# Pooled attention and a maxout layer on one core: block 7's output stage by seven products, its sums on GpSimd, and a rearranged start

## The chip, the cores and the metric

The kernel runs on one core of a Trainium2 chip. A core has five engines that run side by side, each with its own instruction queue, which it works off in order: TensorE (PE: matrix products, results in the memory PSUM; its weight loads are shown as PEld), VectorE (DVE), ScalarE (ACT), GpSimd (POOL) and SyncE (SP, which issues DMA transfers here). They wait for each other by semaphores. PSUM has eight banks of 128 partitions x 512 float32 columns, which the kernel hands out by tags; SBUF is the memory that the other operands live in.

The metric is the time of one execution in device microseconds. A profiled execution gives the span from its first to its last instruction, and a trace of all instructions in between.

## The reference

```python
def _attn_ref(q, k, v):                      # 8 batches, 8 heads, 576 tokens, 64 columns
    k_p = k.reshape(B, H, Sp, pool, D).mean(axis=3)      # pool = 8, Sp = 72
    v_p = v.reshape(B, H, Sp, pool, D).mean(axis=3)
    scores = scale * np.matmul(q, k_p.transpose(0, 1, 3, 2))
    scores = scores - np.max(scores, axis=-1, keepdims=True)
    attn = np.exp(scores)
    attn = attn / (np.sum(attn, axis=-1, keepdims=True) + 1e-09)
    return np.matmul(attn, v_p)

def _moe_ref(x, w1, w2, w3, w_out):          # 4608 tokens, 512 -> 768 -> 512
    h = np.maximum(np.maximum(x @ w1, x @ w2), x @ w3)
    return h @ w_out

x = attn_out.transpose(0, 2, 1, 3).reshape(B * S, H * D)
out = _moe_ref(x, w1, w2, w3, w_out)         # (4608, 512) float32
```

Keys and values are averaged over groups of eight, so the attention is cheap; most of the work is in the layer behind it.

## The kernel before

**The maths.** The hidden layer is computed as x w1 + max(x (w2 - w1), x (w3 - w1), 0). The first part is linear, so w1 w_out is formed once (`linear`, tile `wm`), and the output is x (w1 w_out) + h w_out with h the maximum. `sub_w` makes the differences of the weights in place (L303), in three parts of 256 columns; `turn_w` transposes w1 for `linear`.

**Attention of a batch.** Queries are transposed (`turn_q` on TensorE for the first three batches, step "T", a DMA transpose in SyncE's queue, for batches 3 to 7, L274); pooled keys are transposed into `kz` ("k"); `scores` gives the scores and ScalarE their exponentials (`et`, L197, steps "s"); `values` multiplies by the pooled values (steps "v", five chunks of tokens per batch), and VectorE divides (`rcp` L247, `xn` L249); `turn_x` transposes the result into `xT` (steps "x"), on TensorE up to batch 2 (L231, then a copy, L235), by a DMA transpose in SyncE's queue from batch 3 on (L225).

**The layer.** The 4608 tokens make nine blocks of 512. For blocks 0 to 5, `hidden(n)` computes two products for each of six groups of 128 hidden rows (`pw`, L330; ScalarE's relu L336, VectorE's maximum L338), in two halves of 256 tokens for the first rows of blocks 0 and 1, and `project(n)` makes four tiles of 128 tokens of the output: four matmuls with `wm` (L370), six with w_out (L374), 512 columns each, a copy (L379) and two stores (L383). Each `yield` in these generators is a slot; a written plan says which attention steps of the next batches go into which slot.

The hidden layers of blocks 6, 7 and 8 are computed by `seven(n)`: Strassen's seven products in Winograd's form, on quarters of 256 tokens and half of the columns, for three groups of rows a, b, c. Step "T" in the order there is `fold_x(n)`, which makes the four sums T1 to T4 of x (L566): VectorE for blocks 6 and 7, GpSimd for block 8. The results are collected by VectorE (L679, L682) and ScalarE (L707, L711). `fold_out` makes the sums of the output weights on GpSimd (L596), one after every second product.

`ORDER` is the written order of the last stage, the weave: "1a" is product 1 for rows a, its n-th appearance being block 6, 7 and 8; "s70" and "v70" are attention steps of batch 7; "F" is one slot of `project`, half an output tile. In it stand ten of the twelve tiles of blocks 5 to 7; one more follows, and then the output of block 8, by `out_seven(8)`: seven products of two times five matmuls of 256 columns (L638), with sums `th` of its hidden rows on VectorE (`fold_h`). Block 7's last tile, in two halves, ends the kernel.

**What sets the order.** Every engine's order is the order of the program's text; nothing reorders it. A step waits for data and for a free buffer: PSUM tags have few buffers ("tr" 1, "pw" 3, "att" 2 with two banks each; in the weave "sc" 2, "pa" 2, "bc" 1, "po" 1, "val" 1). SyncE's queue holds output stores and DMA transposes, GpSimd's holds loads, the poolings of keys and values (L136 to L139) and the sums named above.

**The start.** Before block 0 the first batch's attention is written out by hand: `scores4`, `scores2`, two `values`, two `turn_x`, with `turn_w` and `sub_w` between them and dummy matmuls (`heat`).

Of the kernel before, what the change touches and what calls it, by code (L numbers as in the profile page):

```python
# [14 lines left out]
def kernel(  # L15
# [11 lines left out]
    nc = tc.nc  # L27
# [30 lines left out]
    pools = [stage.enter_context(tc.tile_pool(name="psp", bufs=1, space=PSUM))]  # L58
# [124 lines left out]
    def turn_k(b):  # L183
        pkt = keys(b, ATT if len(pools) == 1 else SC)
        for par, evac in enumerate((nc.vector.tensor_copy, nc.scalar.copy)):
            fill_kz(b, par, 0, H, pkt, evac if b > 2 else nc.vector.tensor_copy)
# [50 lines left out]
    def values(b, c0):  # L237
        tag = ATT if len(pools) == 1 else ("val", 1)
        pav = psum([128, 2, 512], F32, name="pav", tag=tag[0], bufs=tag[1])
        for h in range(H):  # L240
            nc.tensor.matmul(  # L241
                pav[:, h // 4, 65 * (h % 4):65 * (h % 4) + 65],
                ets[b][:, h, c0:c0 + 128], vp_all[:, b, h, :],
                start=True, stop=True)
        pv = pav[:, :, 0:260].rearrange("p g (h e) -> p g h e", e=65)
        rcp = sb3.tile([128, 2, 4], F32, name="rcp", tag="rcp")
        nc.vector.reciprocal(out=rcp, in_=pv[:, :, :, 64])  # L247
        xn = sb3.tile([128, 2, 4, D], F16, name="xn", tag="xn", bufs=6)
        nc.vector.tensor_tensor(  # L249
            out=xn, in0=pv[:, :, :, 0:D],  # L250
            in1=rcp.to_broadcast([128, 2, 4, D]), op=ALU.mult)
        return xn

    CHUNKS = ((0, 0), (128, 0), (256, 0), (384, 0), (448, 64))
    ATT = ("att", 2)
    SC = ("sc", 2)
# [6 lines left out]
    def do(b, steps):  # L263

        for name in steps.split():
            i = int(name[1:] or 0)
            if name[0] in "qQ":
                turn_q(b, *QS[i], nc.vector.tensor_copy if name[0] == "Q"  # L270
                       else nc.scalar.copy, TR)
            elif name[0] == "T":
                qTs[b] = sb2.tile([128, 2 * NG, 128], BF16, name="qT", tag="qT")
                nc.sync.dma_start_transpose(  # L274
                    out=qTs[b], in_=qbs[b].rearrange("p hp t d -> p (hp t d)"))
            elif name[0] == "k":
                turn_k(b)
            elif name[0] == "K":
                fold_k(b, nc.vector)
            elif name[0] == "p":  # L280
                pool_v(b, 4 * i, 4 * i + 4, TR, nc.scalar.copy)
            elif name[0] == "s":
                if i == 0:
                    new_et(b)
                (scores if len(pools) == 1 else scores_flat)(b, i)
            elif name[0] == "d":
                sub_w(i)
            elif name[0] == "w":
                turn_w(i, nc.scalar.copy if i % 2 else nc.vector.tensor_copy)
            elif name[0] == "v":  # L290
                xns[b, i] = values(b, CHUNKS[i][0])
            else:
                turn_x(b, *CHUNKS[i], xns[b, i], ATT if len(pools) == 1 else SC,
                       nc.vector.tensor_copy if name[0] == "X" else nc.scalar.copy)
# [4 lines left out]
    def sub_w(i):  # L299

        part = slice(256 * i, 256 * i + 256)
        for t in w_sb[1:]:
            nc.vector.tensor_tensor(out=t[:, :, part], in0=t[:, :, part],  # L303
                                    in1=w_sb[0][:, :, part], op=ALU.subtract)
# [42 lines left out]
    def hidden(n):  # L347
# [3 lines left out]
        if halves:  # L351
            for c0 in (0, NB // 2):
                for jc in range(3):
                    yield from hidden_part(n, jc, c0, c0 + NB // 2, hT)
# [5 lines left out]
    def project(n):  # L360
        hT = hTs[n]
        for mm in range(4):
            m = 4 * n + mm
            last = m == TOK // 128 - 5
            osb = sb3.tile([128, C], F32, name="osb", tag="osb", bufs=5)
            for c in ((slice(0, C // 2), slice(C // 2, C)) if last else (slice(0, C),)):
                tag = PW if len(pools) == 1 else (PO, SC, PA)[max(0, m - (TOK // 128 - 7))]
# [20 lines left out]
    wm = psum([128, 512], F32, name="wm", tag="tr", bufs=1)  # L388
# [8 lines left out]
    pkp0 = psum([128, 6, D], F32, name="pkp", tag="pw", bufs=3)  # L397
# [24 lines left out]
    turn_q(0, 0, 5, nc.vector.tensor_copy, PW)  # L422
    turn_q(0, 5, 9, nc.scalar.copy, ATT)
    pkt0 = [keys(0, PW) for _ in range(2)]
# [4 lines left out]
    def scores4(h):  # L429
        psc = psum([128, 4, 256], F32, name="psc4", tag="att", bufs=2)  # L430
        for i in range(4):
            score(0, h + i, psc[:, i, :], 0, 0, 4)
        exp(ets[0][:, h:h + 4, 0:256], psc[0:Sp])

    def scores2(h):
        psc = psum([128, 2, 512], F32, name="psc2", tag="att", bufs=2)
# [6 lines left out]
    turn_q(0, 9, 14, nc.vector.tensor_copy, PW)  # L443
    turn_q(0, 14, 18, nc.vector.tensor_copy, PW)
    pool_v(0, 0, 4, PW, nc.vector.tensor_copy)
    scores4(4)
    pool_v(0, 4, 6, PW, nc.vector.tensor_copy)
    pool_v(0, 6, 8, PW, nc.vector.tensor_copy)
    scores2(0)
    xn0 = [values(0, c0) for c0, _ in CHUNKS[:2]]  # L450
    heat(1)
    turn_x(0, 0, 0, xn0[0], PW)
    scores2(2)
    turn_w(0, nc.scalar.copy)
    turn_x(0, 128, 0, xn0[1], PW, nc.vector.tensor_copy)
    sub_w(0)
    scores2(4)
    turn_w(1, nc.vector.tensor_copy)
    scores2(6)


    nc.vector.memset(kz_all[1], 0.0)
    xns[0, 0], xns[0, 1] = xn0

    FOLDS = (3, 4, 5, 6, 7, 8, 9, 11)

    def block(n, plan, parts, folds=()):

        for slot, _ in enumerate(part for stage in parts for part in stage(n)):
# [5 lines left out]
            if folds and slot in FOLDS:  # L475
# [3 lines left out]
    block(0, {0: [(0, "v2")], 1: [(0, "v3 d1")], 2: [(0, "x2")],  # L479
              3: [(0, "x3 w2")], 4: [(0, "v4")], 6: [(0, "x4")],  # L480
              8: [(0, "w3")], 9: [(0, "d2")], 12: [(0, "w4")], 13: [(0, "w5")],
# [3 lines left out]
              32: [(1, "v1 x0")], 33: [(1, "X1 v2")]}, (hidden, project))  # L485
# [7 lines left out]
    def plan1():  # L493
        return {0: [(1, "v3")], 1: [(1, "x2")], 2: [(1, "v4")], 3: [(1, "x3")],
                5: [(1, "x4")],
                6: [(2, "k")], 8: [(2, "q0")], 9: [(2, "q1")], 11: [(2, "q2 s0")],
# [4 lines left out]
                23: [(2, "v4 x3")], 24: [(2, "x4")], 17: [(2, "s6"), (3, "T")]}  # L501

    def plan(n):
# [4 lines left out]
        got[1] = [(b + 1, "T")]  # L508
# [23 lines left out]
    LEAD = {0: [(6, "s0")], 1: [(6, "s1"), (7, "T")], 2: [(6, "s2")], 3: [(6, "s3")],  # L532
# [35 lines left out]
    def fold_x(n):  # L568

        x, t = halves(n), turns(n)  # L570
        for part in ([slice(0, 1), slice(1, 2)] if n == LAST else [slice(0, 2)]):
            fold_t(nc.gpsimd if n == LAST else nc.vector,
# [26 lines left out]
    def fold_h(n):  # L599

        th[n] = ld.tile([128, 4, JH, HALF], F16, name="th", tag="ktFalse")
        h = {i: hTs[n][:, JH * (i // 2):JH * (i // 2) + JH,
                       HALF * (i % 2):HALF * (i % 2) + HALF] for i in range(4)}
        fold_t(nc.vector, h, [th[n][:, i] for i in range(4)])

    def out_seven(n):
# [6 lines left out]
        def store(e, j, c):  # L613
            for u in range(2):
                b, g = divmod(2 * (4 * n + 2 * j) + u, NG)
                dst = out[S * b:S * b + S, :].rearrange("(r g) c -> r g c", g=NG)
                e.dma_start(out=dst[:, GS[g]:GS[g + 2] + 1:4, c],
                            in_=o[64 * u:64 * u + 64, j, :, c])

        def product(i, m):  # L620
            of = "B" if i == 2 else "C" if i in (4, 7) else "A"
            if i in FIRST:
                tag = {"A": PA, "B": SC, "C": BC if m == 0 else SC}[of]
                banks[of, m] = psum([128, 2, HALF], F32, name=f"o{of}", tag=tag[0],
                                    bufs=tag[1])
            p = banks[of, m][:, 0]
            za, zb = PRODUCTS[i]
            for r in range(5):
                c = slice(128 * m, 128 * m + 128)
                if isinstance(zb, str):  # L630
                    z = int(zb[1]) - 1
                    left = turns(n)[:, z, r, c] if r < 2 else th[n][:, z, r - 2, c]
                else:
                    at = HALF * (zb % 2) + 128 * m
                    left = (xT[:, 2 * (zb // 2) + r, NB * n + at:NB * n + at + 128] if r < 2
                            else hTs[n][:, JH * (zb // 2) + r - 2, at:at + 128])
                right = out_s(int(za[1]))[:, r] if isinstance(za, str) else out_w(za, r)
                nc.tensor.matmul(p, left, right, start=(i in FIRST and r == 0), stop=(r == 4),  # L638
                                 skip_group_check=True)
            done.add((i, m))  # L640

            def copy(j, c):
                nc.scalar.copy(out=o[:, j, m, c], in_=p)

            def plus(j, c, p):
                nc.vector.tensor_tensor(out=o[:, j, m, c], in0=o[:, j, m, c], in1=p,
                                        op=ALU.add)

            if i in (1, 5, 6, 3):
                copy(i in (5, 3), lo if i in (1, 3) else hi)  # L650
            elif i == 2:
                plus(0, lo, p)
                if m:
                    store(nc.gpsimd, 0, lo)
            elif i == 4:
                plus(0, hi, p)
                if m:
                    store(nc.sync, 0, hi)
            if i in (5, 7) and (12 - i, m) in done:
                plus(1, hi, banks["C", m][:, 0])  # L660
            if i in (5, 7, 3) and all((z, m) in done for z in (5, 7, 3) for m in range(2)):
                store(nc.sync, 1, slice(0, C))

        return product

    def seven(n):
# [19 lines left out]
        def product(i, g):  # L686
# [3 lines left out]
            if not done:  # L690
                hTs[n] = new_hT()
# [30 lines left out]
        k7 F F T v62 1a 1b F s70 s71 6a 6b 2a 7a s72 v63 5a s73 F 2b 5b 4a s74 3a  # L722
        s75 F s76 7b 1c s77 v64 s78 4b 6c F v70 2c 5c 7c 3b F v71 3c F 4c 1a 1b T F
        v72 2b F 2a 6b 6a 7a F v73 5a F v74 3a 5b 4a F 1c F 6c 7b 3b T F 5c 4b F 7c
        1a 2c 2a 4c 6a 3c F 5a 7a 1b 2b 3a 6b 4a 1c 2c 5b 6c 7b 3b F 4b 5c F 7c 3c F
        4c
    """

    def weave():

        products, seen, sums = {}, {}, fold_out()
        for name in ORDER.split():
            if name == "F":
                next(tiles)
            elif name[0] in "ksvx":
# [34 lines left out]
    tiles = (t for n in range(5, LAST) for t in project(n))  # L770
    weave()
    next(tiles)
    next(tiles)
# [37 lines left out]
```

The softmax here doesn't subtract the row's maximum and nothing guards it: scores larger than these inputs give would overflow.

## Time and profile before

| | |
|---|---|
| median of 13 runs | 238.13 us |
| lowest and highest of them | 233.06 and 243.7 us |
| the profiled execution | 233.06 us |
| its span | 231.2 us |
| granted TensorE clock, mean | 1.000 |

The page's section 2 shows the span in 40 slices, each digit the busy share in tenths:

```profile
PE   7787999999999999999999999999999999999992
DVE  3669756037434342624263336258679887897730
ACT  2356434755774577237723772475686535465330
POOL 7665202999915999999996999910243442920020
DMA  6999999999499868998997899972431537311236
```

A slice is 5.8 us. TensorE is busy nearly everywhere; VectorE is busiest in the weave, from the 28th slice on; GpSimd pools keys and values until the 27th and makes sums after it.

In the lines below, a group is "line engine operation out<-in"; times of windows and of the timeline count from the span's start; square brackets hold an engine's idle time before an instruction and what ended it.

### The profile page before, as it was taken

To read this page: it belongs to the slowest core of one execution; us is meant where nothing else is said; L and a number is where in the kernel's file an instruction comes from. 1 tells how busy PE (TensorE), PEld (TensorE's weight loads), DVE (VectorE), ACT (ScalarE), POOL (GpSimd) and SP (SyncE) were. 2 spreads that over 40 slices of the span, in tenths; PEclk is the share of its full clock that TensorE was granted. 3 is DMA by queue.
4 is the path that set the end of the run, shared out by engine and by line. 5 is a ranking of instruction groups with operands and counts; after the bars stand their busy time and mean duration, and the time that the engine had idled before them with its cause. 6 is when DMAs were issued, how large, how long until landed. Compare 5 with 4: busy or idle time off the path is not lost.

```text
span 231.2 us, 4547 instructions
## 1 busy us (share of the span) xinstructions
PE 221.2 (96%) x1766; PEld 137.0 (59%) x1767; DVE 128.2 (55%) x237; ACT 120.3 (52%) x215; POOL 137.9 (60%) x113
## 2 busy tenths in 40 slices
PE   7787999999999999999999999999999999999992
PEld 2575745557656555545554555455677667786682
DVE  3669756037434342624263336258679887897730
ACT  2356434755774577237723772475686535465330
POOL 7665202999915999999996999910243442920020
PEclk9999999999999999999999999999999999999999
DMA  6999999999499868998997899972431537311236
GB/s 181 205 196 197 212 202 212 177 186 227 72 204 166 177 149 139 183 174 195 148 184 174 152 213 171 152 180 49 79 72 25 112 70 105 70 23 45 67 73 181
DMA packets 47174, 33.53 MB, mean 145 GB/s; under 512 B 27313, under 2 KB 41905, under 8 KB 47153
## 3 DMA queue, kind: packets, MB, share of 16 engines
q0 software_dynamic: 16960, 16.98, 45.7%
q1 hardware_dynamic: 30032, 16.13, 33.7%
q8 instruction: 14, 0.23, 0.4%
q10 hardware_dynamic: 160, 0.13, 0.2%
q14 instruction: 8, 0.06, 0.1%
HBM read 34.60 MB, written 9.44 MB: 190 GB/s over the span
## 4 chain that ended last, share of the span: by engine, by line
PE 88%; DVE 3%; DMA 3%; ACT 1%; issue 1%; POOL 1%; POOLq 0%; DVEq 0%
PE pw L330 26%; PE po L374 18%; PE po L370 12%; PE pA L701 7%; PE psc L192 5%; PE pav L241 4%; PE pC L701 3%; DMA vt<-in_v_dram 3%; PE pm L317 2%; PE oA L638 2%; PE pxt L231 2%; PE pB L701 2%; PE pkt L174 1%; DVE mw L303 1%; PE oC L638 1%
## 5 line engine op out<-in xcount | busy, mean ns | idle before, releaser
L330 PE MATMUL pw<-xT,mw 128*128 128x512 f16 (+1 forms) x336 | 73.1, 349 | 0.3 <-DVE xT L235 0.3
L338 DVE TENSOR_TENSOR hT<-t,pw 128x512 f16<-128x512 f16 (+1 forms) x42 | 25.5, 609 | 39.6 <-ACT et L197 26.9
L374 PE MATMUL po<-mwo,hT 128*128 128x512 f16 (+1 forms) x198 | 46.8, 372 | 0.0
L379 ACT COPY osb<-po 128x512 f32<-128x512 f32 (+1 forms) x32 | 18.5, 579 | 42.0 <-PE po L374 41.2
L330 PEld LDWEIGHTS <-mw 128*128 128x128 f16 x336 | 28.9, 98 | 19.2 <-issue 0.8
L197 ACT ACTIVATE et<-psc 72x576 f16<-72x576 f32 (+2 forms) x54 | 35.3, 660 | 6.3 <-PE psc L192 6.1
L136 POOL TENSOR_TENSOR half<-vt 72x2048 f32<-72x2048 f16 x7 | 28.4, 4061 | 13.8 <-DMA vt<-in_v_dram 13.4
L370 PE MATMUL po<-wm,xT 128*128 128x512 f16 (+1 forms) x132 | 33.0, 372 | 0.0
L336 ACT ACTIVATE t<-pw 128x512 f16<-128x512 f32 (+1 forms) x42 | 22.5, 536 | 15.4 <-PE pw L330 13.6
L249 DVE TENSOR_TENSOR xn<-pav,rcp 128x512 f16<-128x512 f32 x40 | 27.6, 691 | 1.4
L374 PEld LDWEIGHTS <-hT 128*128 128x128 f16 x198 | 18.4, 98 | 16.2
L137 POOL TENSOR_TENSOR half<-half 72x1024 f32<-72x1024 f32 (+1 forms) x13 | 27.2, 2096 | 1.0
L192 PEld LDWEIGHTS <-kz 128*128 128x128 bf16 x191 | 17.5, 98 | 13.7 <-DVE kz L179 0.4
L192 PE MATMUL psc<-qT,kz 128*128 128x320 bf16 (+2 forms) x168 | 22.4, 246 | 0.4 <-DVE kz L179 0.3
L241 PEld LDWEIGHTS <-et 72*128 72x128 f16 x320 | 15.4, 98 | 8.3 <-issue 0.6
L707 ACT CAST pad<-pA 128x512 f16<-128x512 f32 x27 | 15.3, 587 | 8.4 <-PE pA L701 6.0
L136 POOL TENSOR_TENSOR half<-ktFalse 96x1536 f32<-96x1536 f16 x6 | 18.6, 3098 | 0.3
L247 DVE RECIPROCAL rcp<-pav 128x8 f32<-128x8 f32 x40 | 8.2, 204 | 17.8 <-PE pav L241 17.6
L241 PE MATMUL pav<-vp,et 72*128 72x65 f16 x320 | 17.2, 194 | 0.6 <-ACT et L197 0.6
L370 PEld LDWEIGHTS <-xT 128*128 128x128 f16 x132 | 11.9, 98 | 9.0
L682 DVE SCALAR_TENSOR_TENSOR hT<-pad 128x512 f16<-128x512 f16 x18 | 14.4, 810 | 1.8 <-ACT pad L711 1.4
L701 PEld LDWEIGHTS <-sw 128*128 128x128 f16 x144 | 13.7, 98 | 2.7
(102 smaller groups left out, 274.2 us busy)
## 6 DMA issues: line engine op xcount, KB each, us to landing
out_dram<-osb SPq DMA_DIRECT2D x62, 128.0 KB, 2.5
ktFalse<-in_k_dram POOLq DMA_DIRECT2D x7, 576.0 KB, 6.9
qb<-in_q_dram POOLq DMA_DIRECT2D x7, 576.0 KB, 13.9
vt<-in_v_dram POOLq DMA_DIRECT2D x7, 576.0 KB, 11.3
mw<-in_moe_w_dram POOLq DMA_DIRECT2D x9, 256.0 KB, 10.0
ktTrue<-in_k_dram SPq DMA_DIRECT2D x3, 384.0 KB, 5.0
mwo<-in_moe_w_out_dram POOLq DMA_DIRECT2D x1, 768.0 KB, 12.9
qb<-in_q_dram POOLq DMA_DIRECT2D x2, 288.0 KB, 7.8
```

The costliest lines, as they stand in the source:

```text
L136: e.tensor_tensor(out=f, in0=t[:, :, 0:4, :], in1=t[:, :, 4:8, :], op=ALU.add)
L137: e.tensor_tensor(out=f[:, :, 0:2, :], in0=f[:, :, 0:2, :], in1=f[:, :, 2:4, :], op=ALU.add)
L192: nc.tensor.matmul(out, kz_all[b % 2][:, f % 2, h, :], qTs[b][:, n + i0:n + i1, 64 * (h % 2):64 * (h % 2) + 64], start=True, stop=True)
L197: nc.scalar.activation(out=out, in_=in_, func=FT.Exp, scale=1.0 / 64.0)
L241: nc.tensor.matmul(pav[:, h // 4, 65 * (h % 4):65 * (h % 4) + 65], ets[b][:, h, c0:c0 + 128], vp_all[:, b, h, :], start=True, stop=True)
L249: nc.vector.tensor_tensor(out=xn, in0=pv[:, :, :, 0:D], in1=rcp.to_broadcast([128, 2, 4, D]), op=ALU.mult)
L330: mm = nc.tensor.matmul(pw, w_sb[wi][:, kc, bass.ts(jc, 128)], xT[:, kc, col], start=(kc == 0), stop=(kc == KCH - 1))
L336: nc.scalar.activation(out=t, in_=pw, func=FT.Relu)
L338: nc.vector.tensor_tensor(out=hT[:, jc, c0:c1], in0=t, in1=pw, op=ALU.max)
L370: nc.tensor.matmul(po, xT[:, kc, bass.ts(m, 128)], wm_sb[:, kc, c], start=(kc == 0), stop=False)
L374: nc.tensor.matmul(po, hT[:, jc, bass.ts(mm, 128)], wo_sb[:, jc, c], start=False, stop=(jc == JCH - 1))
L701: mm = nc.tensor.matmul(p[:, w], a[:, kc, bass.ts(g, 128)], b[:, kc, :], start=(i in FIRST and w + kc == 0), stop=(w + kc == 2), skip_grou ...
```

## The change

Five things are changed together.

1. Block 7's output is also made by `out_seven`, within the weave, with both halves of 128 tokens in one call ("o1" to "o7"), so that its copies and additions cover 512 columns. `project` makes blocks 5 and 6 alone, and block 6's last tile, in two halves, ends the kernel.
2. GpSimd makes block 7's sums: `fold_x(7)`, and `fold_h(7)` (step "H") in twelve instructions of 128x256. Block 8's hidden rows get a tile of their own.
3. `ORDER` is written anew, and block 5's weight sums (`FOLDS`) come a slot earlier.
4. The query transposes "T" of batches 4 to 7 come three slots earlier.
5. The start is rearranged: its own pool of PSUM ("att" with three buffers, "one" with two), closed before `turn_w`; scores and values in another order; the first subtraction in pieces; `turn_w`, `sub_w` and the clearing of the second `kz` in later slots of block 0; one dummy matmul less. Block 0's hidden halves come in another order, v3 of batch 1 moves from block 1 into block 0, q0 of batch 2 a slot earlier, and `turn_x` of batch 1 uses the tag "tr".

```diff
     def values(b, c0):
-        tag = ATT if len(pools) == 1 else ("val", 1)
+        tag = (ATT0, ATT, ("val", 1))[len(pools) - 1]
...
-                turn_x(b, *CHUNKS[i], xns[b, i], ATT if len(pools) == 1 else SC,
+                turn_x(b, *CHUNKS[i], xns[b, i], TR if b == 1 else ATT,
...
-            for c0 in (0, NB // 2):
-                for jc in range(3):
-                    yield from hidden_part(n, jc, c0, c0 + NB // 2, hT)
+            parts = {}
+            for p in ("00 00 01 01 10 10 11 11 02 02 12 12" if n == 0 else
+                      "00 00 01 01 02 02 10 10 11 11 12 12").split():
+                if p not in parts:
+                    c0 = int(p[0]) * NB // 2
+                    parts[p] = hidden_part(n, int(p[1]), c0, c0 + NB // 2, hT)
+                next(parts[p])
+                yield
...
     scores2(0)
-    xn0 = [values(0, c0) for c0, _ in CHUNKS[:2]]
-    heat(1)
-    turn_x(0, 0, 0, xn0[0], PW)
+    xn0 = [values(0, CHUNKS[0][0])]
     scores2(2)
+    xn0.append(values(0, CHUNKS[1][0]))
+    turn_x(0, 0, 0, xn0[0], ONE)
+    scores2(4)
+    sub_w(0, 0, 1, (1,))
+    turn_x(0, 128, 0, xn0[1], ONE, nc.vector.tensor_copy)
+    sub_w(0, 0, 1, (2,))
+    sub_w(0, 1, 2)
+    scores2(6)
+    first.close()
+    pools.append(stage.enter_context(tc.tile_pool(name="psp", bufs=1, space=PSUM,
+                                                  reuse_waits="tile")))
     turn_w(0, nc.scalar.copy)
-    turn_x(0, 128, 0, xn0[1], PW, nc.vector.tensor_copy)
-    sub_w(0)
-    scores2(4)
-    turn_w(1, nc.vector.tensor_copy)
-    scores2(6)
-
-
-    nc.vector.memset(kz_all[1], 0.0)
...
-    block(0, {0: [(0, "v2")], 1: [(0, "v3 d1")], 2: [(0, "x2")],
-              3: [(0, "x3 w2")], 4: [(0, "v4")], 6: [(0, "x4")],
-              8: [(0, "w3")], 9: [(0, "d2")], 12: [(0, "w4")], 13: [(0, "w5")],
+    block(0, {0: [(0, "v2")], 1: [(0, "v3")], 3: [(0, "x2 x3 w1 v4")], 6: [(0, "x4 d1")], 9: [(0, "w2")], 10: [(0, "d2")], 11: [(0, "w3")], 12: [(0, "w4")], 14: [(0, "w5 z")],
...
-              32: [(1, "v1 x0")], 33: [(1, "X1 v2")]}, (hidden, project))
+              32: [(1, "v1 x0")], 33: [(1, "X1 v2 v3")]}, (hidden, project))
...
-        got[1] = [(b + 1, "T")]
+        got[18] = [(b + 2, "T")]
...
     def fold_h(n):
 
-        th[n] = ld.tile([128, 4, JH, HALF], F16, name="th", tag="ktFalse")
         h = {i: hTs[n][:, JH * (i // 2):JH * (i // 2) + JH,
                        HALF * (i % 2):HALF * (i % 2) + HALF] for i in range(4)}
-        fold_t(nc.vector, h, [th[n][:, i] for i in range(4)])
+        if n < LAST:
+            t = ld.tile([128, 4, JH, HALF], F16, name="th", tag="ktFalse")
+            th[n] = [t[:, i] for i in range(4)]
+            for r in range(JH):
+                fold_t(nc.gpsimd, {i: h[i][:, r] for i in h}, [t[:, i, r] for i in range(4)])
+            return
...
-        k7 F F T v62 1a 1b F s70 s71 6a 6b 2a 7a s72 v63 5a s73 F 2b 5b 4a s74 3a
-        s75 F s76 7b 1c s77 v64 s78 4b 6c F v70 2c 5c 7c 3b F v71 3c F 4c 1a 1b T F
-        v72 2b F 2a 6b 6a 7a F v73 5a F v74 3a 5b 4a F 1c F 6c 7b 3b T F 5c 4b F 7c
-        1a 2c 2a 4c 6a 3c F 5a 7a 1b 2b 3a 6b 4a 1c 2c 5b 6c 7b 3b F 4b 5c F 7c 3c F
-        4c
+        k7 1a F F 2a T 1b v62 s70 F s71 s72 6a F s73 v63 5a 7a s74 s75 v64 F s76 4a
+        s77 3a s78 6b 2b 7b 1c v70 2c 5b T F 6c v71 3b F 5c 4b F v72 7c 3c 1a F 1b
+        4c v73 2a 2b 6b 6a F v74 5a 7a F 3a F T 1c 4a 5b 2c 6c 7b 3b F 5c 4b F 1a 7c
+        2a 3c 6a 4c H 1b 2b 5a 6b 7a 3a o1 1c 4a o2 5b 6c 7b 2c o6 4b 3b 5c o5 7c o7
+        4c 3c o3 o4
...
+            elif name == "H":
+                fold_h(LAST - 1)
+                outs = out_seven(LAST - 1)
+            elif name[0] == "o":
+                outs(int(name[1]), 0, 1)
...
-    tiles = (t for n in range(5, LAST) for t in project(n))
+    tiles = (t for n in range(5, LAST - 1) for t in project(n))
     weave()
-    next(tiles)
-    next(tiles)
     outs = out_seven(LAST)
     fold_h(LAST)
```

## The prediction, made before the changed kernel ran

> **What bounds the kernel now.** I read the page first, then a table of windows cut at the stages, then the TensorE timeline of the windows that have idle time, then GpSimd's timeline in the last stage.
>
> From the page:
>
> ```profile
> span 231.2 us, 4547 instructions
> PE 221.2 (96%) x1766; PEld 137.0 (59%) x1767; DVE 128.2 (55%) x237; ACT 120.3 (52%) x215; POOL 137.9 (60%) x113
> PE 88%; DVE 3%; DMA 3%; ACT 1%; issue 1%; POOL 1%; POOLq 0%; DVEq 0%
> ```
>
> TensorE is the bound, and the chain that ended last runs through it for 88%. Where the other 12% lie, the windows tell (us, then busy time and count of PE, PEld, DVE, ACT, POOL, then clock, DMA share, GB/s):
>
> ```profile
> 0.00:10.00 10.00, 7.64 (x48) 3.69 (x48) 4.76 (x10) 1.74 (x2) 7.83 (x17) 1.00 0.88 192
> 10.00:26.00 16.00, 13.19 (x170) 10.52 (x168) 12.23 (x29) 9.47 (x18) 8.84 (x12) 1.00 1.40 198
> 46.00:60.00 14.00, 13.27 (x145) 9.63 (x143) 8.15 (x18) 7.87 (x17) 13.68 (x9) 1.00 1.01 197
> 60.00:161.70 101.70, 101.70 (x737) 53.95 (x735) 44.03 (x82) 56.02 (x96) 79.33 (x44) 1.00 0.90 160
> 161.70:217.10 55.40, 55.40 (x452) 39.22 (x450) 45.00 (x75) 31.18 (x56) 20.24 (x28) 1.00 0.33 65
> ```
>
> From 60 to 217.1 us TensorE never rests, so there only less matrix work helps, and each new wait costs its full length. Idle time stands in the prologue and at two places near 52 and 59 us. The timeline (start, length, line, in brackets the idle time before and its releaser):
>
> ```profile
> 15.82 0.40 PE L231 MATMUL pxt<-identh,xn 128*128 128x128 f16 x4 [0.15 <-DVE xn L249]
> 17.96 0.38 PE L309 MATMUL pwt<-identh,mw 128*128 128x128 f16 x4 [0.59 <-ACT w1T L310]
> 21.01 0.40 PE L231 MATMUL pxt<-identh,xn 128*128 128x128 f16 x4 [0.22 <-DVE xn L249]
> 22.18 0.40 PE L231 MATMUL pxt<-identh,xn 128*128 128x128 f16 x4 [0.34 <-DVE xn L249]
> 24.88 0.40 PE L231 MATMUL pxt<-identh,xn 128*128 128x128 f16 x4 [0.36 <-DVE xn L249]
> 52.52 0.60 PE L330 MATMUL pw<-xT,mw 128*128 128x256 f16 x4 [0.26 <-DVE xT L235]
> 59.45 0.44 PE L167 MATMUL pqt<-ident,qb 128*128 128x128 bf16 x5 [0.34 <-ACT qT L169]
> ```
>
> The ends of matmuls are modelled some 0.17 us late, so the true hole is that much longer: 0.42 us at 52.52 and 0.51 at 59.45, from start to start less the work.
>
> **The output stage of block 7.** Removed: four tiles of 10 matmuls of 512 columns. In the chain six of them (L374) take 1.29 to 1.30 us, so 40 x 0.216 = 8.64 us. Added: 7 products x 2 x 5 = 70 matmuls of 256 columns; ten of them (L638) take 1.09 us in the chain, so 70 x 0.109 = 7.62. Gain 1.02 us, all in a stage without idle time. ScalarE gives up four copies of 512 columns and gets four of the same size (0.585 us each, L379): nothing. VectorE gives up block 7's four token sums (0.41 to 0.89, L566) and gets three additions of 512 columns from PSUM (0.69, as L679): nothing within 0.4 us, and it is busy 45.0 of 55.4 us. The new stores (8 DMAs for 8) stand ahead of block 8's and go out some 10 us before the end. Block 6's last tile ends the kernel in two halves as block 8's last tile did, so the 4.1 us from TensorE's last matmul to the span's end stay. One cover is thin: block 8's hidden sums (VectorE, 0.55 each) now queue behind o4's addition (0.69), so T2 is there 0.2 + 0.69 + 1.1 = 2.0 us after o4; TensorE has four plain products (2.18) until then. Without it the end moves by what is missing. The earlier weight sums in block 5 fall where VectorE is busy 44.0 of 101.7 us: nothing.
>
> **GpSimd's new work** is the price. It gets eight sums for block 7's inputs and twelve for its hidden rows (th), 20 instructions of 128x256, behind the weight sums and block 8's eight sums, in one queue. What such a row costs:
>
> ```profile
> 197.09 0.67 POOL L566 TENSOR_TENSOR pad<-xT 128x256 f16<-128x256 f16 x1
> 197.83 1.00 POOL L566 TENSOR_TENSOR pad<-xT,pad 128x256 f16<-128x256 f16 x1
> 199.42 1.12 POOL L566 TENSOR_TENSOR pad<-xT,pad 128x256 f16<-128x256 f16 x1
> 203.12 0.67 POOL L596 TENSOR_TENSOR so<-mwo,so 128x256 f16<-128x256 f16 x1
> ```
>
> From 197.09 to 203.12 it did eight: 6.03 us, 0.754 each; undisturbed they follow each other at 0.63. The long two overlap VectorE's maximum (L682). First the inputs' sums: from v70 to block 7's product 6b, which reads T2, TensorE has 13 products of 0.435, four half-tiles (4.32) and four values groups (1.08), 11.1 us; the transpose of v70 lands some 4.5 us after v70's start, six sums take 4.5, with 0.4 between, so 1.7 us are to spare: no cost. Then the chain to product 6 of the new stage ("o6" in the order), counted from v74. TensorE: v74 0.27, 30 products 13.05, half-tiles 2 x 0.865 + 2 x 1.295 = 4.32, o1 and o2 2.18, so o6 would start at 19.8 us and read the last th piece at 20.3. GpSimd: xn is there at 1.4, but SyncE's two stores stand ahead until 2.05 (0.79 for ScalarE's copy, 1.2 for two issues, as at 183.23); the transpose lands in 2.4 (DMA view, 170 to 200 us): 4.45; the first sum starts 0.4 later; eight sums 6.0: 10.9; five weight sums at 0.65: 14.1; ten th sums at 0.63 plus two meetings with L682 at 0.4: 21.2. Late by 0.9, with the semaphore 1.0 us; behind the waiting matmul stands all of TensorE's rest, so nothing hides it. Ends: all 18 sums undisturbed at 0.63, 19.4 us, no wait; all at 1.12 (row 199.42), 28.3 us, a wait of 8.0. I take 1.0, since the row of eight is the same work beside the same neighbours.
>
> The Trainium skill speaks against this move: "SBUF — State Buffer", section "SBUF: two separate sides", says that GpSimd and a VectorE instruction with two SBUF inputs share a port pair as an exclusive lock, the later one blocked for the whole of the other. The rows here show 0.33 to 0.50 us for a meeting; by the lock it would be up to 0.69, and the two th meetings would make the wait an estimated 1.6 us instead of 1.0.
>
> **The prologue.** I laid the new order out by hand with this trace's steps (four transposes 0.22, a values group 0.27, two score pairs 0.28, a half hidden group 0.44; reciprocal to xn's end 0.93; a copy 0.58 on ScalarE, 0.42 on VectorE; a subtraction of half size 0.34 to 0.42, half of L303's 0.68). To 15.82 nothing differs. Then the last scores start at 16.92 (18.18 before), since nothing waits for a w1T copy; the first hidden group at 17.82 (18.46), the third values group at 18.33 behind the last exp, hidden groups at 18.60, 19.31, 19.75; x2's transposes 20.19; x3's 21.15, 0.74 us idle behind xn, because both now stand together; the fifth hidden group 22.21 behind ScalarE's copy; then 22.65, 23.08, 23.74, 24.42 and 25.08 (two short waits for the subtraction), and the second 512-column group starts at 27.95 with the same work done. Before it started at 28.61: gain 0.66 us. The dummy matmul taken out (0.22) stood in a hole. Ends: -3.3 us if every hole from 15.7 to 25.2 closed (from start to start less the work they are 3.1, plus 0.2), and +0.5 if one more VectorE step of 0.69 fell into the x3 wait. I take the layout's 0.66.
>
> **Blocks 0 and 1.** v3 moves ahead of block 1's first hidden group: its 0.27 us fills the hole of 0.42. q0 goes one slot earlier, so the copy that q1 waits for (0.69) has two slots of 0.44: the hole of 0.51 shrinks to 0.09. Gain 0.69; ends 0 and 0.93.
>
> **The query transposes** of batches 4 to 7 go three slots earlier in SyncE's queue, ahead of two stores each. Such an issue took 2.05 to 2.25 us, once 9.8 (129.57). What is behind it is stores, five buffers deep, so it costs nothing; the x transposes come later. If a load were late, these stores would be late by 2 to 10 us, and ScalarE's copies next. Before, the 9.8 us stood ahead of batch 5's x transposes.
>
> **Sum:** 231.2 - 1.02 + 1.0 - 0.66 - 0.69 = 229.8 us; with 1.9 around it 231.7, against 233.06 of the profiled execution: -1.4 us. That execution is the shortest of the thirteen shown, 5.07 below their median of 238.13. I keep this distance: 238.1 - 1.4 = **236.7 us**.
>
> **Rivals.** (1) No change: the prologue's layout is off by its small end (0) and the o6 wait is 1.7 us (0.77 a sum): -1.02 + 1.7 - 0.69 = 0.0, 238.1 us. For it: 0.754 is measured and the new stage has more meetings. Against: the holes at 52 and 59 are plainly filled. (2) Slower: GpSimd becomes the bound before o6. At 0.90 us a sum the 18 sums take 16.2 us where I have 13.1: a wait of 4.1, net +1.7, 239.8 us; it decides from 0.81 us on, where the wait passes the 2.4 us of gains. For it: 1.00 and 1.12 among the rows, 1.17 at 172.8. Against: 22 of 28 such rows took 0.67. (3) More than forecast: the thirteen runs reach from 233.06 to 243.70, and the transposes moved out of the loads' way take that spread with them; then the median comes to lie at 231.7. For it: the 9.8 us issue, ahead of x transposes that block 5 needs. Against: in the profile no TensorE wait comes from it.
>
> **How the numbers follow.** Forecast 0.55, (1) 0.15, (2) 0.18, (3) 0.12. The forecast's own range is 235 to 238; (3) takes the low end to 231.3; of (2) the part to 239.2 is kept. About 0.3% (0.7 us) is what a measurement can tell from no change: faster 0.67, same 0.15, slower 0.18.
>
> **What would show it.** Right: idle time before the first matmul of product 6 that reads th, released by GpSimd, of 0.5 to 1.5 us, and no other in the last stage; holes at 52 and 59 under 0.2 us; the second 512-column group at 28.0; TensorE's column work 1 us less. Wrong: no wait at o6 (then 1 us better), a wait of over 2.4 us there (then slower), or new waits on VectorE in the weave, for which I found none.

## The result and the profile after

| | before | after |
|---|---|---|
| median of the runs of the comparison, us | 236.76 | 236.57 |
| profiled execution, us | 233.06 | 236.13 |
| its span, us | 231.2 | 234.2 |

The ratio after to before is 1.0117, 95% interval 1.0097 to 1.0137: the change makes the kernel 1.2% slower, where the prediction had it 1.4 us faster. The medians look alike because that of before holds disturbed executions, which the ratio leaves out; the spans, 3.0 us apart, agree with the ratio.

The page of after: span, busy times, the granted clock in 40 slices, and the chain's shares by engine.

```profile
span 234.2 us, 4629 instructions
...
PE 221.4 (95%) x1796; PEld 140.7 (60%) x1796; DVE 127.9 (55%) x237; ACT 120.5 (51%) x216; POOL 153.6 (66%) x133
...
PEclk9999999999999999999999999999999999997999
...
PE 86%; DVE 3%; POOL 3%; DMA 2%; issue 2%; ACT 1%; SPq 0%; DVEq 0%
```

Two things are new: GpSimd stands in the chain with 3%, where it had 1%, and one slice of the clock is not full. The windows of after (columns as in the prediction) show in which stage:

```profile
46.00:60.00 14.00, 13.87 (x155) 10.50 (x154) 8.26 (x19) 8.49 (x19) 13.68 (x9) 1.00 1.01 198
60.00:160.00 100.00, 100.00 (x720) 52.75 (x717) 43.75 (x82) 55.08 (x94) 79.32 (x44) 1.00 0.90 163
160.00:217.00 57.00, 53.70 (x459) 40.45 (x459) 41.21 (x67) 30.36 (x55) 35.89 (x48) 0.97 0.26 52
206.00:210.40 4.40, 1.57 (x13) 1.01 (x11) 1.56 (x3) 0.77 (x2) 4.24 (x8) 1.00 0.00 0
210.40:213.90 3.50, 3.02 (x15) 2.15 (x16) 0.67 (x1) 0.58 (x1) 1.67 (x3) 0.51 0.00 0
```

From 46 to 60 us TensorE gained 0.6 us of work: the holes at 52 and 59 are closed. The stage from 160 us on, which had no idle time before, has 3.3 us of it, all between 206 and 211; and the 3.5 us behind it ran at a clock of 0.51. GpSimd's work there rose from 20.24 to 35.89 us. TensorE's timeline at that place (in brackets the idle time before and its releaser):

```profile
206.80 0.38 PE L680 MATMUL oA<-so,pad 128*128 128x256 f16 x2
207.02 0.27 PE L680 MATMUL oA<-so,th 128*128 128x256 f16 x1
208.26 0.28 PE L680 MATMUL oA<-so,th 128*128 128x256 f16 x1 [0.97 <-POOL th L577]
210.88 0.40 PE L680 MATMUL oA<-so,th 128*128 128x256 f16 x1 [2.33 <-POOL th L577]
```

This is product 6 of block 7 ("o6"), at the place the prediction named, waiting piece by piece for th. From start to start, less the work, the two waits are 1.13 and 2.51 us: 3.64 instead of the forecast 1.0. What GpSimd did until then:

```profile
192.75 0.90 POOL L577 TENSOR_TENSOR pad<-xT 128x256 f16<-128x256 f16 x1 [2.93 <-DVE pad L727]
...
198.39 0.67 POOL L577 TENSOR_TENSOR pad<-xT,pad 128x256 f16<-128x256 f16 x1
199.02 0.67 POOL L608 TENSOR_TENSOR so<-mwo,so 128x256 f16<-128x256 f16 x1
199.65 1.11 POOL L608 TENSOR_TENSOR so<-mwo 128x256 f16<-128x256 f16 x1
...
201.47 1.12 POOL L608 TENSOR_TENSOR so<-mwo 128x256 f16<-128x256 f16 x1
...
203.18 1.20 POOL L577 TENSOR_TENSOR th<-hT 128x256 f16<-128x256 f16 x1
...
210.16 0.67 POOL L577 TENSOR_TENSOR th<-hT,th 128x256 f16<-128x256 f16 x1
```

These are eight sums for block 8 (192.75 to 199.02) and five weight sums (to 203.18); the tenth th sum ends at 210.83. GpSimd stands idle before 192.75, and the VectorE row named in the bracket is not what holds it: the transpose of xn landed at 192.54, 0.21 us earlier, and the same 0.21 lies between landing and first sum in the experiments below (191.76 to 191.97 in sums_early, 191.89 to 192.10 in o6_late, 192.90 to 193.11 in dummies). In SyncE's queue (start and length of the issue):

```profile
187.72 1.11 SPq L393 DMA_DIRECT2D out_dram<-osb  x2
188.91 2.43 SPq L227 DMA_TRANSPOSE xT<-xn  x1
```

### The profile page after: what moved, and what is told of

The parts are those of the page before. It is cut to its first block, busy times and chain, and to the rows that moved or that the text cites. A ratio compares the mean times of both kernels' runs of the same rounds, so it can differ in the third digit from the quotient of the medians.

```text
span 234.2 us, 4629 instructions
## 1 busy us (share of the span) xinstructions
PE 221.4 (95%) x1796; PEld 140.7 (60%) x1796; DVE 127.9 (55%) x237; ACT 120.5 (51%) x216; POOL 153.6 (66%) x133
## 4 chain that ended last, share of the span: by engine, by line
PE 86%; DVE 3%; POOL 3%; DMA 2%; issue 2%; ACT 1%; SPq 0%; DVEq 0%
PE pw L335 26%; PE po L384 16%; PE po L380 10%; PE pA L750 6%; PE psc L194 5%; PE pav L243 4%; PE oA L680 3%; PE pC L750 3%; POOL th L577 3%; DMA ktTrue<-in_k_dram 2%; PE pm L322 2%; PE oC L680 2%; PE pB L750 1%; PE pxt L233 1%; PE pqt L169 1%
## 5 line engine op out<-in xcount | busy, mean ns | idle before, releaser
L384 PE MATMUL po<-mwo,hT 128*128 128x512 f16 (+1 forms) x174 | 41.0, 371 | 0.0
L389 ACT COPY osb<-po 128x512 f32<-128x512 f32 (+1 forms) x28 | 16.2, 578 | 36.8 <-PE po L384 34.7
L380 PE MATMUL po<-wm,xT 128*128 128x512 f16 (+1 forms) x116 | 28.9, 371 | 0.0
L384 PEld LDWEIGHTS <-hT 128*128 128x128 f16 x174 | 16.0, 98 | 14.0
L727 DVE TENSOR_TENSOR pad<-pad,pC 128x512 f16<-128x512 f16 x18 | 12.3, 684 | 9.5 <-PE pC L750 9.1
```

What stands on the lines that cost most here:

```text
L380: nc.tensor.matmul(po, xT[:, kc, bass.ts(m, 128)], wm_sb[:, kc, c], start=(kc == 0), stop=False)
L384: nc.tensor.matmul(po, hT[:, jc, bass.ts(mm, 128)], wo_sb[:, jc, c], start=False, stop=(jc == JCH - 1))
```

## The experiments

Ratios are to the kernel before, each with its 95% interval. "Holes" are worked out as in the prediction: start to start less the work.

**Weight sums earlier (sums_early).** Edit:

```
-                if n < LAST and len(mms) % 2:
+                if n < LAST:
                     next(sums, None)
```

> One weight sum is issued on GpSimd after every product, not after every second one; nothing else is changed. In the changed kernel five of these sums (199.02 to 203.18 us) stand between the token sums of block 8 and the hidden sums of block 7, for which product 6 waits 3.64 us. Theory (the step mis-sized was the length of GpSimd's queue before product 6): the hidden sums start some 4.2 us earlier, product 6 waits under 0.3 us, the fall of TensorE's clock after it goes too (about 1.5 us), the span falls from 234.2 to about 229.1 us and the ratio to the kernel before from 1.012 to about 0.990. Rival (the length of the queue is not what matters; GpSimd meets VectorE wherever its sums stand): product 6 waits over 1.0 us still, or other products wait in its place, ratio 1.000 or more.

Measured: 0.9884 (0.9843 to 0.9924), span 228.7 us. Its GpSimd timeline and TensorE's at product 6:

```profile
191.97 1.07 POOL L577 TENSOR_TENSOR pad<-xT 128x256 f16<-128x256 f16 x1 [4.66 <-DVE pad L727]
...
197.78 0.67 POOL L577 TENSOR_TENSOR pad<-xT,pad 128x256 f16<-128x256 f16 x1
198.40 0.67 POOL L577 TENSOR_TENSOR th<-hT 128x256 f16<-128x256 f16 x1
```

```profile
206.19 0.38 PE L680 MATMUL oA<-so,pad 128*128 128x256 f16 x2
206.41 0.65 PE L680 MATMUL oA<-so,th 128*128 128x256 f16 x3
206.90 0.38 PE L680 MATMUL oA<-so,pad 128*128 128x256 f16 x2
```

The weight sums now lie earlier. The windows of the 16.6 us before block 7's first token sum, of after and of this run, show GpSimd (the fifth pair) busy for 5.13 and for 11.10 us:

```profile
161.00:177.60 16.60, 16.60 (x157) 11.98 (x155) 11.93 (x24) 12.05 (x23) 5.13 (x8) 1.00 0.37 69
160.50:177.10 16.60, 16.60 (x157) 11.95 (x155) 12.69 (x24) 12.16 (x23) 11.10 (x16) 1.00 0.37 69
```

So no weight sum is left behind block 8's token sums: th follows them directly, and product 6 waits 0.15 us. The idle time before 191.97 is still there, and at 4.66 us longer than in after. The clock is full at this place. The same instructions stand in another order, and the span is 5.5 us less: 3.5 are the wait, 1.5 the clock, and 0.6 a prologue that was shorter in this execution. The theory holds.

**The hidden sums on VectorE (th_vector).** Edit, in `fold_h` for block 7:

```
-            for r in range(JH):
-                fold_t(nc.gpsimd, {i: h[i][:, r] for i in h}, [t[:, i, r] for i in range(4)])
+            fold_t(nc.vector, h, th[n])
```

> The hidden sums of block 7 run on VectorE in four instructions (as before those of block 8), not on GpSimd in twelve. Theory (GpSimd's queue holds product 6): the wait of 3.64 us and the half clock behind it go, less some 0 to 1 us that VectorE's own queue is late by with 2.2 us more in it: span 229 to 230 us, ratio 0.990 to 0.994. Rival (VectorE has no room there, its subtractions of the hidden stage come late and hold TensorE instead): ratio 1.000 or more.

Measured: 1.0023 (0.9982 to 1.0065), span 232.7 us. Product 6 waits no more, but TensorE has one new wait, and VectorE's timeline says why:

```profile
205.67 1.01 PE L749 MATMUL pC<-pad,mw 128*128 128x256 f16 x4 [2.43 <-DVE pad L726]
```

```profile
201.52 1.02 DVE L577 TENSOR_TENSOR th<-hT 128x768 f16<-128x768 f16 x1
202.58 0.91 DVE L577 TENSOR_TENSOR th<-hT,th 128x768 f16<-128x768 f16 x1
203.41 0.54 DVE L577 TENSOR_TENSOR th<-hT 128x768 f16<-128x768 f16 x1
203.88 0.55 DVE L577 TENSOR_TENSOR th<-hT,th 128x768 f16<-128x768 f16 x1
204.35 0.68 DVE L726 TENSOR_TENSOR pad<-pad,pB 128x512 f16<-128x512 f16 x1
```

The four sums take 2.8 us, the first two stretched beside GpSimd's last weight sums, and the subtractions of the hidden stage come that much later. Some 1.5 us of this span are a half clock behind the new wait (last section). The rival was right, in mechanism and in time: the wait moved to VectorE's reader.

**Work that nobody reads (dummies).** Edit: 15 matmuls of 512 columns on a constant before product 6, into the unused half of oA's tile (`spare`, whose making is left out here).

```
+                if name == "o6":
+                    for _ in range(15):
+                        nc.tensor.matmul(spare[0][:, 1].rearrange("p a c -> p (a c)"),
+                                         warm[:, 0:128], warm, start=True, stop=True)
```

> 15 matmuls of 512 columns on a constant, whose results nobody reads, stand before product 6 of block 7 (15 x 0.213 = 3.2 us at full clock); every wait on GpSimd stays as it is. Theory (the half clock from 210.45 to 213.86 us follows from TensorE's standing idle for 1.1 and 2.5 us): the clock stays full, about 1.5 us less than the changed kernel, span 232.7 us, ratio 1.005. Rival (the clock falls for the work done before, or by chance): the clock falls again, ratio 1.012 or above.

Measured: 1.0075 (1.0022 to 1.0128), span 233.4 us. The windows of this run:

```profile
206.00:211.00 5.00, 4.95 (x33) 3.04 (x33) 2.20 (x4) 1.07 (x2) 4.84 (x8) 1.00 0.00 0
211.00:214.00 3.00, 2.85 (x27) 2.33 (x25) 1.14 (x2) 1.32 (x3) 1.72 (x3) 1.00 0.00 0
```

The wait is as long (3.2 us filled, 0.5 left), the clock stays at 1.00 and the 1.5 us behind are gone. The prologue of this run was 0.6 us longer, so the span shows only 0.8 of it, and the interval overlaps that of after: the clock row supports the theory, the time alone does not prove it. A slow stretch of 3.41 us brings the mean clock of such a span down to 0.993; of the executions that the comparison uses, seven of ten of after have 0.993 or less, and none of seven of this run.

**The front alone (front_only)**: the new prologue, blocks 0 and 1 and query transposes, before the old `ORDER`, `seven`, `fold_h` and `out_seven`.

> The changed kernel's prologue, its plan of blocks 0 and 1 and its later query transposes stand ahead of the hidden and output stages of the kernel before. Theory: the front's gain of 1.07 us (idle in the first 60 us from 10.42 to 9.35 us) and 0.2 us of a dummy matmul reach the end: ratio about 0.9945. Rival (the gain is swallowed in the stage behind, where GpSimd or transposes set the pace): ratio 0.999 to 1.001.

Measured: 0.9918 (0.9876 to 0.9960), span 229.6 us, 1.6 less than before; the forecast 1.3 lies within the interval. The front is a gain and reaches the end.

**Product 6 later (o6_late).** Edit, in `ORDER`:

```
-        2a 3c 6a 4c H 1b 2b 5a 6b 7a 3a o1 1c 4a o2 5b 6c 7b 2c o6 4b 3b 5c o5 7c o7
-        4c 3c o3 o4
+        2a 3c 6a 4c H 1b 2b 5a 6b 7a 3a o1 1c 4a o2 5b 6c 7b 2c 4b 3b 5c 7c o6 4c o5
+        o7 3c o3 o4
```

> Products 6, 5 and 7 of block 7 stand later in the written order, product 6 behind four more products of block 8's hidden stage (4 x 1.1 = 4.4 us); GpSimd's queue stays as in the changed kernel. Theory (product 6 simply stands 3.6 us too early for GpSimd's chain): the wait is under 0.3 us, the clock stays full, span about 229 us, ratio 0.988 to 0.991, as with the weight sums brought forward. Rival (the wait only moves: product 5 behind the eviction of product 6, or block 8's last products): ratio 0.996 or more.

Measured: 1.0045 (1.0011 to 1.0078), span 232.8 us. My expectation had a wrong size: a product of the hidden stage is four matmuls, 0.435 us (as the prediction's own working had it), so the cover was 1.7 us and not 4.4. The timeline:

```profile
206.55 0.60 PE L750 MATMUL pC<-pad,mw 128*128 128x256 f16 x4 [0.40 <-DVE pad L727]
...
211.00 0.28 PE L680 MATMUL oA<-so,th 128*128 128x256 f16 x1 [2.04 <-POOL th L577]
```

The wait shrinks to 2.20 us, a hole of 0.56 opens where the hidden products, now side by side, wait for VectorE, and the clock falls again:

```profile
211.00:214.00 3.00, 3.00 (x17) 2.19 (x18) 1.01 (x2) 0.59 (x1) 1.20 (x2) 0.58 0.00 0
```

Moving the reader opened another hole; moving the writer did not.

**Both remedies (both).**

> Weight sums after every product and product 6 of block 7 later, together. Theory: one remedy is enough, what is left is the 0.15 us that product 6 still waited with the weight sums brought forward, so ratio 0.987 to 0.989. Rival (there is more hidden in this stage): ratio under 0.985; or the two disturb each other: above 0.992.

Measured: 0.9959 (0.9904 to 1.0014), span 229.4 us: worse than the expectation and, by span, 0.7 us more than with the sums alone. Two holes of 0.56 and 0.40 us behind VectorE (L727) stand in the place of the 0.15.

**Query transposes back (turns_back)**, on top of the early weight sums: `got[1] = [(b + 1, "T")]` instead of `got[18] = [(b + 2, "T")]`, and the like in `plan1` and `LEAD`.

> Weight sums after every product, and the query transposes of the later blocks issued where the kernel before issued them (a block later than the changed kernel, those of block 7 in block 5). Theory (the moved transposes are worth nothing): ratio 0.988 as with the weight sums alone, within 0.3%. Rival (the move is a gain, as one case of the prediction has it, or a loss): 0.991 or above, or 0.985 or below.

Measured: 0.9925 (0.9867 to 0.9983), span 229.4 us. The 0.7 us more of span than in sums_early is one hole of 0.80 us, at 124.08, behind ScalarE's `osb`. The interval holds both forecasts: that the move is worth nothing is not refuted, and a gain of some 0.4% is not either.

**The stages alone (weave_only, weave_old_folds, weave_sums)**: the kernel before up to block 5, and the new stages behind it; the second with the old slots of `FOLDS`, the third also with the weight sums after every product.

> The prologue, the plans of blocks 0 to 5 and the query transposes of the kernel before stand ahead of the changed kernel's hidden and output stages. Theory (the loss is wholly in the stage from 160 us on: -1.0 of fewer columns, +3.6 of product 6's wait, +1.5 of the half clock): some 4.1 us slower than before, ratio 1.015 to 1.020. Rival (the wait comes from the new front, where the stage starts earlier or the transposes lie elsewhere): ratio 1.008 or less.

> The kernel before up to block 5, with its own slots for the weight differences of block 5 too, and the changed kernel's hidden and output stages behind it. An earlier run of this pairing with the new slots had, beside product 6's wait of 3.64 us, two holes of 1.65 and 2.19 us at 82 and 106 us, behind late query transposes and late token transposes, which the kernel before did not have at the same places. Theory (those two were DMA transposes that happened to land late, nothing of the stages behind): the wait of 3.64 us comes again, the holes at 82 and 106 us are under 0.3 us, span 233.8 to 235.5 us, ratio 1.010 to 1.018. Rival (they belong to the earlier place of the query transposes in this program and come again): span over 237 us, ratio 1.022 or more.

> As the run before it in this set (front of the kernel before, stages of the changed kernel), with the weight sums after every product. Theory (without the wait the new output stage gives its 1.0 us): faster than the run before it by 3.5 to 5.0 us; if its front has no late transposes, span about 230.3 us, ratio 0.994 to 0.998. Rival (the new stages cost time by something other than GpSimd's queue): less than 2.5 us faster than the run before it.

Measured: 1.0279 (1.0166 to 1.0393), 1.0196 (1.0104 to 1.0287) and 0.9958 (0.9918 to 0.9998); spans 237.8, 239.6 and 230.8 us. The first ratio rests on two executions, the second on three. Product 6 waited 3.64 us in the first, 3.55 in the second and 0.17 in the third: the wait belongs to the new stages whatever front stands before them. Without that wait the new stages are no loss: the rival of weave_sums falls. Of the 7.0 us of span between weave_only and weave_sums 3.5 are this wait and 3.8 two holes (weave_sums' prologue was 0.2 longer):

```profile
82.16 0.44 PE L174 MATMUL pkt<-ident,kp 96*64 96x96 bf16 x6 [1.49 <-POOL kp L139]
...
106.16 1.02 PE L330 MATMUL pw<-xT,mw 128*128 128x512 f16 x4 [2.03 <-DMA xT<-xn]
```

They stand in the front, where all three run the same program up to block 5: 1.65 us at 82 behind late keys and 2.19 at 106 behind late token transposes. weave_sums has neither, so the program's order alone doesn't make them, which speaks against the rival of the second run. They begin with the query transpose issued at 62 us: it landed at 74.69 us in weave_only, at 69.99 in weave_sums and at 71.13 in before, and GpSimd's queue waits for it (10.94 us in weave_only, 7.34 in before) with the key sums behind. In weave_old_folds it landed at 75.71 and the hole was 2.89; but TensorE's clock also fell at 83 us there, so of that span nothing is concluded, and its ratio lies between the two expectations. Why this transpose lands late in some executions is open.

**v74 earlier (v74_early).** Edit, in `ORDER`:

```
-        4c v73 2a 2b 6b 6a F v74 5a 7a F 3a F T 1c 4a 5b 2c 6c 7b 3b F 5c 4b F 1a 7c
+        4c v73 2a 2b 6b v74 6a F 5a 7a F 3a F T 1c 4a 5b 2c 6c 7b 3b F 5c 4b F 1a 7c
```

> In the changed kernel's written order the last values of block 7's attention (v74) stand one hidden product and one token tile earlier, so that its transposes are queued ahead of that tile's two stores; nothing else is moved. In the changed kernel these transposes were issued at 188.91 and landed at 192.54 us, and GpSimd stood idle for 2.5 to 3.0 us until then. Theory (the late start of GpSimd's chain is a second part of the mis-sized step): the token sums of block 8 start 2.4 to 3.0 us earlier, product 6 of block 7 waits 0.6 to 1.3 us and not 3.64, the clock stays full, span 229.5 to 230.5 us, ratio 0.990 to 0.996. Rival (the transposes take their time wherever they stand, or the weight sums fill the gap and the chain ends no earlier): wait over 2.5 us, ratio 1.005 or more.

Measured: 0.9978 (0.9952 to 1.0004), span 232.8 us with a hole of 2.07 us at 102.57 behind late token transposes, as in weave_only. This is the longest of the twelve executions; the others have spans of 230.6 to 232.2 us. Of the stage itself:

```profile
187.61 0.43 PE L243 MATMUL pav<-vp,et 72*128 72x65 f16 x8 [0.86 <-DVE xn L251]
...
210.94 0.28 PE L680 MATMUL oA<-so,th 128*128 128x256 f16 x1 [1.08 <-POOL th L577]
```

Product 6 waits 1.25 us and the clock stays full, as the theory has it; but v74 itself now waits 1.02 us for its single bank, which v73 still holds. I had not counted that. The wait is 2.4 us shorter than in after for two reasons: the transpose landed 4.29 us after v74's start and not 5.63, and by the new order 1.7 us more of TensorE's work stands between v74 and product 6; GpSimd's 23 sums took 0.8 us longer. So the late landing is a second part of the loss, of 1.3 us here.

## Why the prediction was wrong

**The step that failed** is GpSimd's chain to product 6, "Late by 0.9, with the semaphore 1.0 us". Its mechanism and place were right, its size was not: product 6 waited 3.64 us. Counted from v74 in after,

```profile
186.91 0.43 PE L243 MATMUL pav<-vp,et 72*128 72x65 f16 x8
```

the parts of the chain are, each with what it took longer than forecast:

| us from v74 to | forecast | measured | longer by |
|---|---|---|---|
| start of block 8's first sum | 4.85 | 5.84 | 0.99 |
| end of the eight token sums | 10.9 | 12.11 | 0.22 |
| end of the five weight sums | 14.1 | 16.27 | 0.96 |
| end of the ten th sums | 21.2 | 23.92 | 0.55 |

Together 2.7 us; with the forecast 1.0, less 0.1 by which TensorE came to product 6 later, this is the 3.64 measured. The first 1.0 is the transpose: I took 2.4 us from its issue to its landing, and it took 3.63 (188.91 to 192.54). The 2.4 was a median; in the trace of before the transpose issued at 190.60 had taken 4.05. That two stores stand just ahead of it doesn't explain it: those of after issued at 169.80, 178.13 and 182.30 stand behind two stores as well and took 2.44 to 2.45. Why this one landed late is open. The weight sums were priced at an undisturbed 0.65 although they run beside the same VectorE work as the token sums, where 1.11 and 1.12 stand. sums_early took the five weight sums out of the chain altogether (4.2 us), and the wait fell to 0.15; in v74_early the transpose landed 1.3 us sooner after v74, and, with the new order, the wait fell to 1.25.

**A term that was missing**: the half clock behind the wait, 1.5 us. The prediction let a wait cost its own length. The clock was 0.51 from 210.4 to 213.9 us, and full in dummies, where the same wait was filled with work. But not all of after's time hangs on it: three of the ten executions that the comparison uses have a mean clock of 1.00, with spans of 232.3, 234.1 and 234.8 us, and the six at 0.993 have 233.7 to 234.6. What was longer in two of those three no trace shows.

**What held.** The output stage: weave_sums has 0.5 us more of holes than before and a span 0.4 shorter, so 0.9 us of column work went (forecast 1.02); sums_early has the same front and, within 0.1 us, the same sum of holes as front_only, and a span 0.9 us less. Prologue and blocks 0 and 1: the idle time up to 60 us went from 10.42 to 9.35 us, with the dummy matmul (0.22) 1.29 us, forecast 1.35; the holes at 52 and 59 are 0.16 and 0.07. The second 512-column group started at 28.27 us in after and at 27.86 in front_only (forecast 27.95). Transposes: turns_back resolves no effect. The earlier `FOLDS` of block 5 were not tried alone.

**The sum** for after: -1.02 - 1.29 + 3.64 + 1.5 = +2.8 us, measured +3.0. Of the rivals the second comes nearest: its side and its place were right, and the wait was past the 2.4 us from which it decides. Its reason was not: the 18 sums took 13.92 us, 0.77 each and not 0.90. That is the price of rival (1), which made a wait of 1.7 us of it; the transpose (1.0) and the weight sums (1.0) made the rest of the wait, and the clock came on top. My list named the sign itself ("a wait of over 2.4 us there"). That the time of 236.7 us is met to 0.1 us is luck: it carried the distance between profile and median of before, which after doesn't have.

On the lock of the Trainium skill, "SBUF — State Buffer", section "SBUF: two separate sides": from 192 to 211 us in after a meeting cost a sum of 0.67 us between 0.23 and 0.53, and VectorE's maximum (0.69 alone) up to 0.50, so a meeting is paid by either side. Each lies below the 0.69 that I had taken as the most that the lock allows. With 0.69 a meeting I had estimated a wait of 1.6 us; that too is below the measured 3.64, since most of what was missing is in rows I had not priced with meetings, and in the transpose.

## What to carry to other kernels

Where one queue feeds a reader, price every instruction in it with its neighbours, also those that were there before, and start the chain from the late landings on record, not from their median. Before moving the reader back or the work to another engine, which here moved the wait along, look for idle time earlier in the same queue: weight sums put into idle time of GpSimd 30 us and more before product 6 made a loss of 1.2% a gain of 1.2% (0.9884), faster than both kernels.

## What the hardware showed

TensorE's clock fell to half for 3.41 us at waits shorter than that: in after from 210.45 to 213.86 us, at waits of 1.13 and 2.51 us; in weave_old_folds from 83.06, at 2.89 us; in o6_late from 211.45, 0.45 us after the end of a wait of 2.20 us; in th_vector at a single 2.6 us:

```profile
203.00:205.60 2.60, 0.24 (x3) 0.07 (x1) 2.60 (x6) 0.92 (x2) 0.07 (x1) 0.94 0.00 0
205.60:208.70 3.10, 3.03 (x15) 2.10 (x15) 2.00 (x4) 0.00 (x0) 0.00 (x0) 0.50 0.02 5
```

Not every execution showed it: weave_only had the same 3.64 us of waits and a hole of 2.19 us at a full clock, v74_early one of 2.07, and of the runs of th_vector that the comparison uses five have a clock of 1.00 and spans of 231.1 to 231.8 us, four one of 0.992 to 0.996 and spans of 232.6 to 233.7. The Trainium skill, "TensorE: Matmul & The Clock Gate", section "What's actually happening", says that the clock falls after an idle window of about 3.4 us and comes back after a busy one, and that the window runs freely, so that the point of change varies from run to run. The length of the slow stretch and the variation agree with it; but waits of 2.20 to 2.89 us, with work right before and behind, were enough here, and why was not tried.
